# Sharing the casts of v between two engines, one bank pair for batch 1's kv, and another order of stores and loads in SyncE's queue

## The chip, the cores and the metric

The kernel runs on one core of one Trainium2 chip. A core has five engines that run side by side, each through its own list of instructions in order: TensorE (PE in the profile; its weight loads are PEld), VectorE (DVE), ScalarE (ACT), GpSimd (POOL) and SyncE (SP), which issues most of the DMAs. They wait for each other by semaphores. The metric is the device time of one execution in microseconds (us), and the number quoted is the median of several executions.

## What is computed

The program is a linear attention followed by a two-layer network over every token. There are 8 batches of 8 heads, 576 tokens and a head width of 64; the model width is 512 and the hidden width 2048. Cut to what matters, the reference is:

```python
def phi(x): return np.where(x > 0, x, np.exp(x) - 1.0) + 1.0
q_p, k_p = phi(q), phi(k)
kv  = np.einsum('bhsd,bhse->bhde', k_p, v)      # one 64x64 matrix a head
z   = np.sum(k_p, axis=2)
num = np.einsum('bhsd,bhde->bhse', q_p, kv)
den = np.einsum('bhsd,bhd->bhs', q_p, z)[..., None] + 1e-06
x   = (num / den)                                # tokens x 512
h   = x @ w_in                                   # 512 -> 2048
g   = 0.5*h*(1 + tanh(sqrt(2/pi)*(h + 0.044715*h**3)))
out = g @ w_out                                  # 2048 -> 512
```

All inputs and the output are float32 in memory. The kernel computes its matrix products in bf16 and sums them in float32.

## The kernel before

**Tiling.** Of every batch the first 512 tokens form one group; the last 64 tokens of all 8 batches together form a ninth group. `iteration(j)` does the network for group j: 16 steps "h" (one 128-wide block of the hidden width each, four matmuls of 128x512, L385, and a gelu on ScalarE, L395) and 16 or more steps "o" (four or two matmuls into one of four token tiles, L726). Each step has a slot number. The attention of later batches is laid between these steps: `at(j, slot, fn)` notes that fn is to be written out after the given slot of iteration j, and `run` calls it there. So the order of the instructions on every engine is the order in which the Python code writes them; nothing reorders them later.

**Attention of one batch.** q and k go through phi: an exp on ScalarE (L219), a `max(x + 1, 1)` on VectorE (L227), and a minimum of the two (L233). v is cast to bf16 (`cast_v_paired`, L238) into a tile `vp` that has a column of ones beside each head's 64 columns, so that the product with k also gives the sum of k. The kv matmuls (`kv_paired`, L249) run over J = 9 pieces of 64 tokens, for four blocks u of two heads each. Their results stand in PSUM and are copied out into `kvbd`, a block-diagonal bf16 tile (`kv_evac`, L261). Then for each of four chunks of 128 tokens, q (transposed) is multiplied by kvbd (`nab`, L265, tile `n_ps`), VectorE divides (L282, L283), and the result x is transposed into `xt`, the operand of the h steps.

**PSUM.** It has two pools here: `bank` hands out one of six single banks, and `pair_of_banks` the one pair of two neighbouring banks, which is one tile. The pair is used by `nab` for n_ps, and by some batches for kv. Whoever takes it next has to wait until the tile before has been read.

**The start.** `first_batch` prepares batch 0 with nothing beside it but a few matmuls that keep TensorE going (`keep_warm`). v's four blocks come in two halves, `halves[0]` and `halves[1]`; both are cast by VectorE. Kv of the first half goes to two single banks, kv of the second half to the pair, from which VectorE copies the upper 64 partitions and ScalarE the lower 64.

**Batch 1** is prepared by `plan_second` within iteration 0: the transposes of q at slot 23 with two copies by ScalarE (L536), the cast of v by VectorE followed by a cast of a piece of w_out (L145), kv at slot 27 in two single banks, one copied out by VectorE, the other by ScalarE, and n from slot 29 on.

**Loads and stores.** Loads go through SyncE's queue, in the order written. The staging tiles of q, k, v and of the two weight matrices share one pool of seven buffers. Ahead of everything stand the loads for batches 0 to 3 and the weights; later batches' loads are written out by `at`. Transposes by DMA (of q, and of x from batch 2 on) go through the same queue. Stores of the output tiles `o_sb` are issued by ScalarE (L715); the two of group 0 wait until slot 2 of iteration 1.

Of the kernel before, what the change touches and what calls it, by code (L numbers as in the profile page):

```python
# [15 lines left out]
def kernel(  # L16
# [16 lines left out]
    nc = tc.nc  # L33

    B, H, S, D = q.shape
    d_model, d_ff = moe_w_in.shape
    P = 128
# [4 lines left out]
    NP = H // 2  # L42
# [66 lines left out]
    def load_all_pairs(name, src, b):  # L109
        ld_tile(name, b)  # L110
        load_pairs(name, src, b)
# [58 lines left out]
    load_w_out(2, slice(2, 4))  # L170
    load_w_out(3, slice(0, 2))
    load_w_out(3, slice(2, 4))
    for b in (2, 3):
        load_q(b)
        load_all_pairs("k", k, b)
        load_all_pairs("v", v, b)

# [54 lines left out]

    def cast_v_paired(b, us, fn):
        fn(  # L238
            out=vp_paired(b)[:, :, us, 0:D].rearrange("p j u d -> p u j d"),
            in_=ld["v", b][:, us].rearrange("p u (j d) -> p u j d", d=D),  # L240
        )

    def kv_paired(b, ii, kv_of):
# [168 lines left out]
    def first_batch():  # L412
        w_ps = bank("w_ps", [P, 512])

        def keep_warm(n):
            for _ in range(n):
                nc.tensor.matmul(w_ps, lhsT=warm[:, 0:P], rhs=warm)  # L417

        qt = pt.tile([P, C, NP, P], BF16, name="qt")
        qs = (slice(0, 4), slice(4, 8))  # L420

        def transpose_q(s, fn):
            t_ps = bank("t_ps", [P, C, 2, P], BF16)
            for i in range(2):
                for c in range(C):
                    h = 4 * s + 2 * i
                    nc.tensor.transpose(
                        t_ps[:, c, i, :], phi["q", 0][:, c, h : h + 2, :], ident
                    )
            fn(out=qt[:, :, 2 * s : 2 * s + 2, :], in_=t_ps)  # L430

        keep_warm(18)
        for s in range(2):
            for n, hs in (("q", qs[s]), ("k", halves[s])):
                exp_of(n, 0, hs)
                linear_of(n, 0, hs)
                least_of(n, 0, hs)
        transpose_q(0, nc.scalar.copy)
        keep_warm(8)
        transpose_q(1, nc.scalar.copy)  # L440
        keep_warm(5)
        for ii in range(2):
            cast_v_paired(0, halves[ii], nc.vector.tensor_copy)
        kv_ps = [bank("kv_ps", [P, E]) for _ in range(2)]
        kv_paired(0, 0, lambda a, ii: kv_ps[a])
        for a, fn in enumerate((nc.vector.tensor_copy, nc.scalar.copy)):
            kv_evac(0, slice(2 * a, 2 * a + 1), kv_ps[a].rearrange("p (i e) -> p i e", i=1), fn)
        keep_warm(1)
        kv_ps = pair_of_banks("kv_ps")
        kv_paired(0, 1, lambda a, ii: kv_ps[:, a, 0:E])  # L450
        kv_evac(0, slice(1, 4, 2), kv_ps[:, :, 0:E], nc.vector.tensor_copy, nc.scalar.copy)
        for fs in (slice(0, 128), slice(128, 256), slice(256, 512)):
            cast_w_in(0, nc.gpsimd.tensor_copy, fs)
        cast_w_in(1, nc.gpsimd.tensor_copy, slice(256, 512))
        for i in range(2, 4):
            cast_w_in(i, nc.gpsimd.tensor_copy)
        for i in range(2):
            cast_w_out(i, nc.gpsimd.tensor_copy)

        xts[0] = pt.tile([P, NP, MAIN], BF16, name="xt")  # L460
        x = {0: x_tile()}

        def t(c, blocks=range(NP)):
            transpose_x(x[c], xt_chunk(0, c), nc.scalar.copy, blocks)

        def h(m, c, blocks=range(KM)):
            h_begin(0, m, slice(P * c, P * (c + 1)), blocks)

        first, second = range(2), range(2, 4)
        nab_half(x[0], qt[:, 0], 0)  # L470
        nab_half(x[0], qt[:, 0], 1)
        x[1] = nab(qt[:, 1], 0)
        t(0, first)
        h_begun[0][0] = bank("h_ps", [P, MAIN])
        nc.tensor.matmul(h_begun[0][0], lhsT=warm[:, 0:P], rhs=warm, skip_group_check=True)
        t(0, second)
        for m in range(2):
            h(m, 0, first)
        x[2] = nab_in_banks(qt[:, 2], 0)
        h(0, 0, second)  # L480
        t(1)
        h(1, 0, second)
        x[3] = nab(qt[:, 3], 0)
        cast_w_in(1, nc.vector.tensor_copy, slice(0, 256))
        h(2, 0)
        h(3, 0)
        t(2)
        for m in range(3):
            h(m, 1)
        t(3)  # L490
        gelu_table()
        h(3, 1)
        for c in (2, 3):
            for m in range(4):
                h(m, c)
# [16 lines left out]
    def plan_second():  # L512
        b = 1
        x = {}

        def maps():
            for n in "qk":
                exp_of(n, b)
            cast_w_out(2, nc.scalar.copy, slice(0, 2))
            for n in "qk":  # L520
                linear_of(n, b)
            for n in "qk":
                least_of(n, b)

        def transpose_q():
            qts[b] = pt.tile([P, C, NP, P], BF16, name="qt")
            for s in range(2):
                t_ps = bank("t_ps", [P, 2, NP, P], BF16)
                for c in range(2):
                    for i in range(NP):  # L530
                        nc.tensor.transpose(  # L531
                            t_ps[:, c, i, :],
                            phi["q", b][:, 2 * s + c, 2 * i : 2 * i + 2, :],
                            ident,
                        )
                nc.scalar.copy(qts[b][:, 2 * s : 2 * s + 2], t_ps)  # L536

        def casts():
            cast_v_paired(b, slice(0, NP), nc.vector.tensor_copy)
            cast_w_out(2, nc.vector.tensor_copy, slice(2, 4))  # L540

        def kv():
            kv_ps = [bank("kv_ps", [P, 2, E]) for _ in range(2)]
            for ii in range(2):
                kv_paired(b, ii, lambda a, ii: kv_ps[a][:, ii, :])
            for a, fn in enumerate((nc.vector.tensor_copy, nc.scalar.copy)):
                kv_evac(b, slice(2 * a, 2 * a + 2), kv_ps[a], fn)

        def last_w_out():
            for m, fn in enumerate((nc.gpsimd.tensor_copy, nc.scalar.copy) * 2):  # L550
                cast_w_out(3, fn, slice(m, m + 1))
            gelu_table()

        def n(c):
            x[c] = (nab_in_banks if c == 1 else nab)(qts[b][:, c], b)

        def t(c):
            if c == 0:
                xts[b] = pt.tile([P, NP, MAIN], BF16, name="xt")
            transpose_x(x[c], xt_chunk(b, c), nc.scalar.copy)  # L560

        at(0, 15, maps)
        at(0, 23, transpose_q)
        at(0, 23, casts)
        at(0, 27, kv)
        at(0, 27, last_w_out)
        at(0, 29, n, 0)
        at(0, 29, n, 1)
        at(0, 32, n, 2)
        at(0, 32, t, 0)  # L570
        at(0, 33, t, 1)
        at(0, 33, n, 3)
        at(0, 34, t, 2)
        at(0, 34.5, t, 3)
        at(0, 35, h_begin, b, 0, slice(0, 3 * P))
        at(0, 35, h_begin, b, 0, slice(3 * P, MAIN))
# [4 lines left out]
    def plan_third():  # L581
        def n(c):
            transposed_x(2, c, nab(qts[2][:, c], 2))

        for i, name in enumerate("qk"):
            at(1, 2 + i, linear_of, name, 2)
            at(1, 7, exp_of, name, 2)
        at(1, 4, cast_v, 2)
        at(1, 7, gelu_table)
        at(1, 9, least_q, 2)  # L590
        at(1, 10, load_all_pairs, "k", k, 4)
        at(1, 11, least_of, "k", 2)
        at(1, 16, kv_in_pair, 2)
        for c in range(C):
            at(1, 18 + 2 * c, n, c)
# [15 lines left out]
    def plan_prepare(j):  # L611

        b = j + 2
        has_k = b + 1 < B
        at(j, 10 if j == 2 else 4, cast_v, b)
        if has_k:
            at(j, 14 if j == 2 else 12, linear_of, "k", b + 1)
        at(j, 13, linear_of, "q", b)
        at(j, 15, exp_of, "q", b)
        at(j, 20, least_q, b)  # L620
        if has_k:
            at(j, 15, exp_of, "k", b + 1)
            at(j, 22, least_of, "k", b + 1)
# [74 lines left out]
    def finish(j, t, o_ps):  # L698
# [12 lines left out]
        if t % 2 == 1:  # L711
            ov = out[j * S : j * S + MAIN, :].rearrange("(p c) f -> p c f", c=C)[:, t - 1 : t + 1]

            def store():
                nc.scalar.dma_start(out=ov, in_=o_sb)  # L715

            if j == 0:
                at(1, 2, store)
            else:
                store()  # L720

    def o_mm(o_ps, g, t, ms, fs=slice(0, d_model), half=None):
        for m in ms:
# [59 lines left out]
        plan_rest(m)  # L783
    for b in range(3, B + 1):
        plan_attention(b)
    at(1, 26, load_all_pairs, "v", v, 4)
    at(1, 26, load_q, 4)
    for b in range(5, B):
        at(b - 3, 1, load_all_pairs, "k", k, b)
# [40 lines left out]
```

## Time and profile before

| what | value |
|---|---|
| device time, median of 4 runs | 283.76 us (283.67 to 284.01) |
| the profiled execution's own time | 283.77 us |
| its span, first to last instruction | 282.0 us |
| TensorE busy | 273.7 us |
| ScalarE busy | 164.4 us |
| VectorE busy | 102.7 us |
| GpSimd busy | 15.0 us |
| moved by DMA | 53.81 MB, 191 GB/s on average |

The profile is one execution on the chip. Times within it count from its first instruction. In a line of the timeline the first number is the start, the second the duration, then come engine, line of the kernel, operation, output<-input, shapes, how many, and in brackets the idle time of the engine just before and what ended it. In a line of waits the numbers are the total in us, how often, and the longest. The chain that ended last is followed back from the last instruction through whatever released each step. Records of a few matmuls are missing, so a count of 3 can stand for 4.

### The profile page before, as it was taken

The page shows a single profiled execution, that of the slowest core. Times are in us where ns is not written, and L with a number is a line of the kernel's source. Part 1 is how long each engine was busy: PE and PEld are TensorE (multiplying, and loading weights), DVE is VectorE, ACT ScalarE, POOL GpSimd, SP SyncE. Part 2 cuts the span into 40 slices and gives each one's busy share as a digit, 9 for nine tenths or more (in the row PEclk, how much of TensorE's full clock was granted, in tenths as well). Part 3 has the DMA queues.
Part 4 walks back from the last instruction along what each step waited for, and adds up shares of the span by engine and source line. Part 5 has one row for each costly group of instructions (what it writes and reads, how often), then busy time and mean ns, then how long its engine had stood idle before and what let it go on. Part 6 is the DMA issues. An engine that isn't in the chain of part 4 may idle for free.

```text
span 282.0 us, 5115 instructions
## 1 busy us (share of the span) xinstructions
PE 273.7 (97%) x2151; PEld 135.1 (48%) x2181; DVE 102.7 (36%) x177; ACT 164.4 (58%) x224; POOL 15.0 (5%) x21
## 2 busy tenths in 40 slices
PE   8899999999999999999999999999999999999995
PEld 3584455445444544454445444544444444444444
DVE  3850286434955750356034640350124001400001
ACT  4778878785987915692569346833682364026400
POOL 3148200000000000000000000000000000000000
PEclk9999999999999999999999999999999999999999
DMA  7999999977999767916794540056305300430022
GB/s 246 401 406 397 411 402 403 404 253 219 188 358 294 269 170 208 379 28 167 193 390 106 152 131 2 2 151 172 88 2 149 112 2 0 118 108 0 0 77 74
DMA packets 59590, 53.81 MB, mean 191 GB/s; under 512 B 35760, under 2 KB 45360, under 8 KB 59568
## 3 DMA queue, kind: packets, MB, share of 16 engines
q1 hardware_dynamic: 56784, 44.58, 50.8%
q10 hardware_dynamic: 2784, 8.91, 8.8%
q8 instruction: 17, 0.28, 0.4%
q14 instruction: 5, 0.04, 0.0%
HBM read 36.70 MB, written 9.44 MB: 164 GB/s over the span
## 4 chain that ended last, share of the span: by engine, by line
PE 93%; DMA 3%; issue 1%; SPq 1%; DVE 1%; ACT 0%
PE h_ps L385 44%; PE o_ps L726 44%; DMA v_x<-in_v_dram 3%; PE n_ps L323 1%; PE n_ps L249 1%; PE kv_ps L249 1%; PE n_ps L265 1%; PE t_ps L378 1%; SPq L95 1%; SPq L100 0%; PE t_ps L531 0%; DVE vp L238 0%; DVE x L368 0%; DVE kvbd L261 0%; DVE o_sb L687 0%
## 5 line engine op out<-in xcount | busy, mean ns | idle before, releaser
L726 PE MATMUL o_ps<-w_out_sb,g 128*128 128x512 bf16 (+2 forms) x588 | 126.0, 367 | 1.6 <-issue 0.9
L385 PE MATMUL h_ps<-xt,w_in_sb 128*128 128x512 bf16 (+1 forms) x556 | 113.2, 359 | 0.5 <-issue 0.2
L395 ACT ACTIVATE g<-h_ps 128x512 bf16<-128x512 f32 x144 | 84.6, 599 | 36.3 <-PE h_ps L385 34.9
L385 PEld LDWEIGHTS <-w_in_sb 128*128 128x128 bf16 x628 | 58.5, 98 | 64.6
L726 PEld LDWEIGHTS <-g 128*128 128x128 bf16 x608 | 57.4, 98 | 63.4
L687 ACT COPY o_sb<-o_ps 128x512 f32<-128x512 f32 (+1 forms) x19 | 10.8, 576 | 65.4 <-PE o_ps L726 52.3
L687 DVE COPY o_sb<-o_ps 128x512 f32<-128x512 f32 (+1 forms) x19 | 12.2, 646 | 50.3 <-PE o_ps L726 45.5
L282 DVE RECIPROCAL r<-n_ps 128x6 f32<-128x6 f32 (+2 forms) x43 | 8.2, 192 | 60.9 <-PE n_ps L323 55.4
L227 DVE TENSOR_SCALAR k_p<-k_x 128x2304 bf16<-128x2304 f32 (+1 forms) x9 | 11.0, 1222 | 24.5 <-DMA k_x<-in_k_dram 24.5
L283 DVE TENSOR_TENSOR xs<-n_ps,r 128x384 bf16<-128x384 f32 (+1 forms) x30 | 17.5, 584 | 1.0
L219 ACT ACTIVATE k_e<-k_x 128x2304 bf16<-128x2304 f32 (+1 forms) x9 | 17.1, 1903 | 0.9 <-DMA k_x<-in_k_dram 0.9
L219 ACT ACTIVATE q_e<-q_x 128x2048 bf16<-128x2048 f32 (+1 forms) x9 | 15.5, 1720 | 3.0 <-DMA q_x<-in_q_dram 2.9
L227 DVE TENSOR_SCALAR q_p<-q_x 128x2048 bf16<-128x2048 f32 (+1 forms) x9 | 9.9, 1103 | 13.2 <-DMA q_x<-in_q_dram 13.2
L385 PE MATMUL h_ps<-xt_rest,w_in_sb 128*128 128x512 bf16 x63 | 13.9, 379 | 0.1
L233 DVE TENSOR_TENSOR q_p<-q_p,q_e 128x2048 bf16<-128x2048 bf16 (+1 forms) x9 | 9.9, 1102 | 6.9 <-ACT q_e L219 6.8
L408 ACT ACT_TABLE_LOAD x9 | 11.5, 1283 | 0.2
L233 DVE TENSOR_TENSOR k_p<-k_p,k_e 128x2304 bf16<-128x2304 bf16 (+1 forms) x9 | 11.0, 1221 | 1.2 <-ACT k_e L219 1.0
L238 DVE CAST vp<-v_x 128x2304 bf16<-128x2304 f32 (+1 forms) x9 | 11.0, 1224 | 0.5 <-DMA v_x<-in_v_dram 0.3
L417 PE MATMUL w_ps<-warm 128*128 128x512 bf16 x31 | 9.7, 477 | 1.2 <-DVE warm L181 1.2
L219 ACT ACT_TABLE_LOAD x8 | 10.3, 1283 | 0.1
L139 POOL CAST w_in_sb<-w_st 128x512 bf16<-128x512 f32 (+2 forms) x6 | 7.6, 1271 | 15.0 <-DMA w_st<-in_moe_w_in_dram 15.0
L283 DVE TENSOR_TENSOR x<-n_ps,r 128x512 bf16<-128x512 f32 (+1 forms) x13 | 7.9, 609 | 0.4
(50 smaller groups left out, 76.1 us busy)
## 6 DMA issues: line engine op xcount, KB each, us to landing
out_dram<-o_sb ACTq DMA_DIRECT2D x16, 512.0 KB, 3.6
k_x<-in_k_dram SPq DMA_DIRECT2D x7, 1152.0 KB, 7.0
v_x<-in_v_dram SPq DMA_DIRECT2D x7, 1152.0 KB, 11.9
q_x<-in_q_dram SPq DMA_DIRECT2D x6, 1024.0 KB, 11.9
w_st<-in_moe_w_in_dram SPq DMA_DIRECT2D x3, 1024.0 KB, 13.6
q_x<-in_q_dram SPq DMA_DIRECT2D x4, 512.0 KB, 8.6
w_st<-in_moe_w_out_dram SPq DMA_DIRECT2D x2, 1024.0 KB, 12.5
w_st<-in_moe_w_out_dram SPq DMA_DIRECT2D x4, 512.0 KB, 11.2
```

What stands on the lines that cost most here:

```text
L219: nc.scalar.activation(o, i, AF.Exp)
L227: nc.vector.tensor_scalar(o, i, 1.0, 1.0, op0=ALU.add, op1=ALU.max)
L233: nc.vector.tensor_tensor(p, p, e, op=ALU.min)
L238: fn(out=vp_paired(b)[:, :, us, 0:D].rearrange("p j u d -> p u j d"), in_=ld["v", b][:, us].rearrange("p u (j d) -> p u j d", d=D),)
L282: nc.vector.reciprocal(r, n_v[heads + (D,)])
L283: nc.vector.tensor_tensor(x_v, n_v[heads + (slice(0, D),)], r[heads + (None,)].to_broadcast(shape + [D]), op=ALU.mult,)
L385: nc.tensor.matmul(h_ps[:, ts], lhsT=w_in_sb[:, c, P * m : P * (m + 1)], rhs=xt[:, c, ts], start=(c == 0), stop=(c == KM - 1), skip_group_ ...
L395: nc.scalar.activation(g[:, m, :], h_ps, AF.Gelu_apprx_tanh)
L408: nc.scalar.preload_act_table_set("gelu_apprx_tanh_and_others")
L417: nc.tensor.matmul(w_ps, lhsT=warm[:, 0:P], rhs=warm)
L687: (nc.scalar.copy if on_scalar else nc.vector.tensor_copy)(dst, src)
L726: nc.tensor.matmul(o_ps, lhsT=g[:, m, P * t : P * (t + 1)], rhs=w_out_sb[:, m, fs], start=(m == 0), stop=(m == MM - 1),)
```

## The change

Five things are altered. The cast of the second half of v of batch 0, and the cast of v of batch 1, are cut by token pieces: VectorE does pieces 0 to 5 and ScalarE pieces 6 to 8; for batch 1 ScalarE's part stands between its two copies of q. ScalarE alone copies out both parts of kv of batch 0's second half. Batch 1's kv takes the bank pair in place of two single banks. The two stores of group 0 are issued by SyncE, behind the load of q of batch 3, and k of batch 3 is loaded behind them. v of batch 3 is loaded in iteration 1 at slot 26, just ahead of v of batch 4; and VectorE's first step on k of batch 5 moves from slot 14 to slot 18 of iteration 2.

```diff
@@ loads ahead of everything
-    for b in (2, 3):
-        load_q(b)
-        load_all_pairs("k", k, b)
-        load_all_pairs("v", v, b)
+    load_q(2)
+    load_all_pairs("k", k, 2)
+    load_all_pairs("v", v, 2)
+    load_q(3)
@@ the cast
-    def cast_v_paired(b, us, fn):
+    def cast_v_paired(b, us, fn, js=slice(0, J)):
         fn(
-            out=vp_paired(b)[:, :, us, 0:D].rearrange("p j u d -> p u j d"),
-            in_=ld["v", b][:, us].rearrange("p u (j d) -> p u j d", d=D),
+            out=vp_paired(b)[:, js, us, 0:D].rearrange("p j u d -> p u j d"),
+            in_=ld["v", b][:, us].rearrange("p u (j d) -> p u j d", d=D)[:, :, js],
         )
@@ first_batch
-        for ii in range(2):
-            cast_v_paired(0, halves[ii], nc.vector.tensor_copy)
+        cast_v_paired(0, halves[0], nc.vector.tensor_copy)
+        cast_v_paired(0, halves[1], nc.vector.tensor_copy, slice(0, 6))
+        cast_v_paired(0, halves[1], nc.scalar.copy, slice(6, J))
...
-        kv_evac(0, slice(1, 4, 2), kv_ps[:, :, 0:E], nc.vector.tensor_copy, nc.scalar.copy)
+        kv_evac(0, slice(1, 4, 2), kv_ps[:, :, 0:E], nc.scalar.copy)
@@ plan_second, transpose_q, casts and kv
                 nc.scalar.copy(qts[b][:, 2 * s : 2 * s + 2], t_ps)
+                if s == 0:
+                    cast_v_paired(b, slice(0, NP), nc.scalar.copy, slice(6, J))
...
-            cast_v_paired(b, slice(0, NP), nc.vector.tensor_copy)
+            cast_v_paired(b, slice(0, NP), nc.vector.tensor_copy, slice(0, 6))
...
-            kv_ps = [bank("kv_ps", [P, 2, E]) for _ in range(2)]
+            kv_ps = pair_of_banks("kv_ps")
             for ii in range(2):
-                kv_paired(b, ii, lambda a, ii: kv_ps[a][:, ii, :])
+                kv_paired(b, ii, lambda a, ii: kv_ps[:, a, E * ii : E * (ii + 1)])
             for a, fn in enumerate((nc.vector.tensor_copy, nc.scalar.copy)):
-                kv_evac(b, slice(2 * a, 2 * a + 2), kv_ps[a], fn)
+                src = kv_ps[:, a, 0 : 2 * E].rearrange("p (i e) -> p i e", e=E)
+                kv_evac(b, slice(2 * a, 2 * a + 2), src, fn)
@@ plan_third, plan_prepare
+        at(1, 3, load_all_pairs, "k", k, 3)
...
-            at(j, 14 if j == 2 else 12, linear_of, "k", b + 1)
+            at(j, 18 if j == 2 else 12, linear_of, "k", b + 1)
@@ finish
-            def store():
+            if j == 0:
+                at(1, 2, nc.sync.dma_start, ov, o_sb)
+            else:
                 nc.scalar.dma_start(out=ov, in_=o_sb)
-
-            if j == 0:
-                at(1, 2, store)
-            else:
-                store()
@@ the later loads
-    at(1, 26, load_all_pairs, "v", v, 4)
+    for b in (3, 4):
+        at(1, 26, load_all_pairs, "v", v, b)
     at(1, 26, load_q, 4)
```

## The prediction

> **What bounds the kernel now.** I read the page's busy shares first, then the chain that ended last, then TensorE's waits, and last the timeline at the two places where batches 0 and 1 are prepared.
>
> ```profile
> span 282.0 us, 5115 instructions
> PE 273.7 (97%) x2151; PEld 135.1 (48%) x2181; DVE 102.7 (36%) x177; ACT 164.4 (58%) x224; POOL 15.0 (5%) x21
> PE 93%; DMA 3%; issue 1%; SPq 1%; DVE 1%; ACT 0%
> ...
> PE kv_ps L249 <- DVE vp L238: 0.7, 2, 0.4
> PE n_ps L359 <- ACT kvbd L261: 0.4, 1, 0.4
> PE t_ps L378 <- DVE x L368: 0.2, 1, 0.2
> ```
>
> TensorE is busy in 97% of the span and is 93% of the chain; the granted clock is 1.0 throughout. Apart from the wait for its first operand's memset, its only waits for another engine (the last three lines) are in the start-up, before 15 us. After that it never stands still, so a microsecond that it gains or loses anywhere passes to the end unchanged. VectorE, ScalarE, GpSimd and the DMAs count only where they make TensorE wait. The start-up, in order of time (start, duration, engine, line):
>
> ```profile
> 3.39 8.39 DMA v_x<-in_v_dram
> ...
> 11.80 0.76 DVE L238 CAST vp<-v_x 128x1152 bf16<-128x1152 f32 x1
> 12.62 0.48 PE L249 MATMUL kv_ps<-vp,k_p 64*64 64x65 bf16 x36 [0.39 <-DVE vp L238]
> 13.16 0.29 DVE L261 CAST kvbd<-kv_ps 64x130 bf16<-64x130 f32 x1 [0.22 <-PE kv_ps L249]
> 13.48 0.26 ACT L261 CAST kvbd<-kv_ps 64x130 bf16<-64x130 f32 x1 [0.67 <-DVE kvbd L261]
> 13.79 0.27 PE L359 MATMUL n_ps<-kvbd,qt 128*128 128x130 bf16 x2 [0.43 <-ACT kvbd L261]
> ```
>
> v's second half lands at 11.78; VectorE casts it; TensorE's kv matmuls wait; then the two copies out of kv's bank pair run one behind the other, ScalarE 0.03 us after VectorE has ended. Batch 1, which has two separate banks today:
>
> ```profile
> 38.47 1.37 DVE L238 CAST vp<-v_x 128x2304 bf16<-128x2304 f32 x1 [0.34 <-DMA v_x<-in_v_dram]
> 39.81 0.69 DVE L145 CAST w_out_sb<-w_st 128x1024 bf16<-128x1024 f32 x1
> 39.89 0.78 PE L249 MATMUL kv_ps<-vp,k_p 64*64 64x65 bf16 x72
> 40.60 1.04 PE L726 MATMUL o_ps<-w_out_sb,g 128*128 128x512 bf16 x3
> 40.79 0.60 DVE L261 CAST kvbd<-kv_ps 64x130 bf16<-64x130 f32 x2 [0.29 <-PE kv_ps L249]
> 40.81 0.54 ACT L261 CAST kvbd<-kv_ps 64x130 bf16<-64x130 f32 x2 [1.09 <-PE kv_ps L249]
> 41.47 0.63 PE L265 MATMUL n_ps<-kvbd,qt 128*128 128x130 bf16 x8
> ```
>
> Here the two engines copy at the same time, end at 41.39 and 41.35, and n of chunk 0 starts at 41.47, where TensorE arrives anyway. Nothing waits, but every step is in time by less than 0.1 us.
>
> **What the Trainium skill says.** "PSUM — Partial Sum Buffer", section "PSUM bank collisions raise a hardware error": two engines may not touch one bank and quadrant of partitions at once, while different banks run clean; the software has to keep them apart. Here the program keeps them apart by whole tile: the trace has the pair's two copies in sequence (13.45, then 13.48), and the copies of two tiles together (40.79 and 40.81). "DMA: Bandwidth & Descriptors", section "Queues, rings and completion order": SP and ACT each own one row of rings on the same 16 DMA engines; each ring is drained in its order, and rows take turns. The trace agrees: the two stores that ScalarE issues at 50.48 and 51.30 land only 6.7 and 7.9 us later, in a stretch where the DMAs move 388 to 428 GB/s for SyncE's loads.
>
> **The change, part by part.** *v of batch 0.* VectorE's f32 casts take 0.761 us for 1152 elements and 1.357 for 2304, so 0.165 + 0.000517 each; ScalarE's (L145) take 0.618 for 512 and 1.029 for 1024, so 0.207 + 0.00080 each. VectorE's six ninths (768) take 0.56: 11.80 to 12.36. ScalarE's 384 take 0.51 behind its qt copy (10.92 + 1.02 = 11.94), so at most to 12.46; the matmuls that read them are the last third. TensorE can start at 12.41; the keep-warm matmul before it (about 0.21, after the first half ends at 12.23) allows 12.44. That is 0.18 earlier than 12.62. The kv copies follow 0.54 after the start: 12.98. Both are ScalarE's now, 2 x 0.264, to 13.51; n at 13.56 instead of 13.79. From there the chain to the transposes (VectorE's r and x) is what it was, and VectorE has 0.29 less to do. So TensorE gains 0.23 us here. W_in is no obstacle (its first casts end 0.6 us before their matmuls).
>
> *v of batch 1.* TensorE then comes to kv at about 39.66. VectorE's 1536 elements take 0.96: 38.47 to 39.43. ScalarE's 768 take 0.82 behind its first qt copy (about 37.6 to 38.5): ready by 39.4 for the last third. So kv starts on arrival. Its second qt copy slips to about 40.3 and is not read until chunk 2, past 43.6. But the next o matmuls need w_out, whose cast starts with its landing, not with VectorE's being free: it stays at 39.81 + 0.69 = 40.50, matmul at 40.55. Of the 0.23 gained only 0.05 is left there, and TensorE reaches n at 41.42.
>
> *Batch 1's kv in the bank pair.* kv ends 0.23 earlier, so VectorE's two copies run 40.56 to 41.16. In the order of the changed program ScalarE's first copy waits for VectorE's last, and n of chunk 0, whose tile is the same bank pair, waits for ScalarE's last copy before its first matmul. ScalarE: 41.16 + 0.03 + 0.54 = 41.73; n at 41.78. Before: 41.47. This new wait is 0.36 us of standing TensorE. Behind it on ScalarE stand two w_out casts, which end about 0.4 later and have 0.3 to 0.5 of room, plus TensorE's own delay. From here on everything follows TensorE, so **the net is 41.78 - 41.47 = +0.31 us**. Bounds: with no start-up gain at all the serial copies give +0.53; with the copies side by side after all, -0.05.
>
> *Stores on SyncE's queue.* Two issues of 0.39 and 0.34 leave ScalarE (50.48 to 51.64), where they lay under TensorE's h work (ScalarE waits 0.68 for TensorE right after): worth nothing, and at most these 0.73 us if ScalarE set the pace there. SyncE now stands from 42.3 until o_sb is filled at 48.4 to 49.0, with k of batch 3 and batch 2's transposes behind. The ring still holds work until about 53.5 then (q issued at 40.43 lands 13.0 later), so the DMAs don't run dry; k of batch 3 lands near 59 as today (42.40 + 16.5), for a cast at 72.01. The transposes wait for VectorE until 59.87 anyway. Cost nothing.
>
> *v of batch 3 later.* It is issued where batch 4's v stood, 73.36 + 0.31 = 73.67, and the two loads behind it (v, q of batch 4) move back by one load, 2.9 us (1.18 MB at some 400 GB/s). The v issued at that place today lands in 5.9 us:
>
> ```profile
> v_x<-in_v_dram SPq DMA_DIRECT2D x1, 1152.0 KB, 5.9
> ...
> 78.08 1.36 DVE L238 CAST vp<-v_x 128x2304 bf16<-128x2304 f32 x1
> 81.41 0.78 PE L249 MATMUL kv_ps<-vp,k_p 64*64 64x65 bf16 x72
> ```
>
> So it lands at 79.57, the cast runs to 80.95, and TensorE needs it at 81.72: 0.7 us of room where there were 2.0. Next in line: batch 4's v near 82.5 for a cast at 85.46, its q near 85 for VectorE at 86.73; batch 3's transposes near 91 (88.1 today) for TensorE at 93.45; k of batch 5 near 94, which is why its VectorE step stands at slot 18 now, behind the attention; ScalarE's exp of it starts at 95.55. The x transposes of 95.39 to 101.3 are wanted at 107.0 and may end a microsecond or two later. The DMA share falls to 0.2 to 0.6 from 96 to 101, where the backlog is worked off. All hidden; cost nothing, and what it costs when the cover is gone is the first rival.
>
> **Sum.** Profiled execution: span 282.0, own time 283.77, so 1.77 around it, which no edit touches. 282.0 + 0.31 = 282.3, own time 284.08; it lies 0.01 above the median 283.76. I predict **284.1 us**. A measurement of this kernel can tell 0.2% (0.57 us) from no change, so this counts as the same.
>
> **Rivals.** *Slower: v of batch 3 late.* If its load shares the engines with the v queued behind it, instead of going first, both land after 5.9 + 2.9 us, near 82.5; cast to 83.8; TensorE stands about 2.2 us at kv, and the time is 286.3. It decides from a landing later than 80.3. For it: only 0.7 us of room, and four transposes just ahead in the queue. Against it: at the start loads issued together land one after another, and the same place gives 5.9 today with a q queued behind.
>
> *The start-up gain is kept.* If the pair's copies do not hold TensorE, the w_out cast still does: -0.05, 283.7. Against it: the 0.67 that ScalarE waits for VectorE in batch 0's pair.
>
> *No gain at the start.* If ScalarE's cast, or its two copies, take what VectorE saved, the whole +0.53 of the serial copies is left: 284.3.
>
> *Faster by over 0.57 us* has no mechanism that I can see: the three waits shown above add up to 1.3 us, and the landing of v at 11.78 fixes most of them.
>
> **Numbers.** The forecast (+0.2 to +0.5) 0.60, no start-up gain 0.12, gain kept 0.10, v late or another transfer late (each microsecond past its room is one of TensorE) 0.16, something faster 0.02. The range from 283.6 to 285.0 leaves out the late v and the faster end; the likeliest case alone is 283.9 to 284.3. Slower by over 0.2%: the 0.16 of late transfers and a tail of the no-gain case, 0.20; faster 0.04; same 0.76.
>
> **What would show it.** Right: kv of batch 0's second half starts near 12.44 and n at 13.56; in batch 1 ScalarE's copies start just after VectorE's end, near 41.2, and a wait of n_ps (L265) for ScalarE's kvbd of 0.3 to 0.5 us appears among TensorE's waits, which has none there now; v of batch 3 lands by 80.3. Wrong: ScalarE's copies beside VectorE's at 40.6; a wait of kv_ps for vp near 81.7; or a wait on transposes at 93 or 107.

## The result, and the profile after

| kernel | median | range | executions |
|---|---|---|---|
| before | 283.78 us | 283.52 to 284.13 | 53 |
| changed | 284.22 us | 283.96 to 284.52 | 35 |

The ratio is 1.0016, with a 95% interval of 1.0012 to 1.0021: a loss of 0.44 us (0.16%), below the 0.2% at which the prediction draws its line, but clearly not zero. The profiled execution took 284.08 us, against 283.77 for that of before. 284.1 was predicted.

The page of the changed kernel:

```profile
span 282.3 us, 5118 instructions
PE 273.9 (97%) x2151; PEld 135.0 (48%) x2181; DVE 102.0 (36%) x176; ACT 165.7 (59%) x227; POOL 15.0 (5%) x21
PE 88%; DMA 5%; DVE 3%; issue 1%; SPq 1%; ACT 0%; ACTq 0%; DVEq 0%
```

and its waits of TensorE (total in us, times, longest):

```profile
PE n_ps L265 <- ACT kvbd L261: 0.5, 1, 0.5
PE n_ps L359 <- ACT kvbd L261: 0.4, 1, 0.4
PE kv_ps L249 <- DVE vp L238: 0.3, 1, 0.3
```

TensorE's busy time is what it was; its share of the chain fell from 93% to 88%, the rest now running through DMAs and VectorE: between 94 and 106 us the chain passes over VectorE's divisions and a transpose of x by DMA, which lands at 106.03, 0.04 us ahead of TensorE's next piece. TensorE loses no time there: at 93.74 and at 107.31 it is as far behind the kernel before (93.45 and 107.01) as it already was at batch 1. Among the waits, the one at kv of the start has shrunk from 0.7 in two pieces to 0.3 in one, and n_ps at L265 waits for ScalarE's kvbd, which it didn't before. The timeline of the changed kernel at the start:

```profile
11.69 0.56 DVE L238 CAST vp<-v_x 128x768 bf16<-128x768 f32 x1
11.73 0.53 ACT L238 CAST vp<-v_x 128x384 bf16<-128x384 f32 x1
...
12.36 0.48 PE L249 MATMUL kv_ps<-vp,k_p 64*64 64x65 bf16 x36 [0.25 <-DVE vp L238]
12.90 0.54 ACT L261 CAST kvbd<-kv_ps 64x130 bf16<-64x130 f32 x2 [0.22 <-PE kv_ps L249]
13.49 0.27 PE L359 MATMUL n_ps<-kvbd,qt 128*128 128x130 bf16 x2 [0.43 <-ACT kvbd L261]
```

The two casts run side by side (0.56 and 0.53 us for the 0.76 of one engine), and n follows at 13.49 instead of 13.79. The timeline around batch 1:

```profile
38.19 0.96 DVE L238 CAST vp<-v_x 128x1536 bf16<-128x1536 f32 x1 [0.35 <-DMA v_x<-in_v_dram]
38.40 0.85 ACT L238 CAST vp<-v_x 128x768 bf16<-128x768 f32 x1
...
39.53 0.70 DVE L145 CAST w_out_sb<-w_st 128x1024 bf16<-128x1024 f32 x1 [0.37 <-DMA w_st<-in_moe_w_out_dram]
39.55 0.78 PE L249 MATMUL kv_ps<-vp,k_p 64*64 64x65 bf16 x72
40.28 1.02 PE L728 MATMUL o_ps<-w_out_sb,g 128*128 128x512 bf16 x3
40.47 0.60 DVE L261 CAST kvbd<-kv_ps 64x130 bf16<-64x130 f32 x2 [0.24 <-PE kv_ps L249]
41.17 0.54 ACT L261 CAST kvbd<-kv_ps 64x130 bf16<-64x130 f32 x2 [1.03 <-DVE kvbd L261]
41.77 0.63 PE L265 MATMUL n_ps<-kvbd,qt 128*128 128x130 bf16 x8 [0.47 <-ACT kvbd L261]
```

ScalarE's copies start 0.10 us after VectorE's have ended, and TensorE stands 0.47 us at n. It begins n at 41.77 instead of 41.47 and keeps this distance of 0.30 to the end of the span (282.3 instead of 282.0). Of the later loads, the DMA issues of SyncE between 75 and 80 us (count, size, us from issue to landing):

```profile
v_x<-in_v_dram SPq DMA_DIRECT2D x1, 1152.0 KB, 8.0
q_x<-in_q_dram SPq DMA_DIRECT2D x1, 1024.0 KB, 15.2
```

and VectorE's timeline:

```profile
79.89 1.36 DVE L238 CAST vp<-v_x 128x2304 bf16<-128x2304 f32 x1 [1.43 <-DMA v_x<-in_v_dram]
90.54 1.23 DVE L227 TENSOR_SCALAR q_p<-q_x 128x2048 bf16<-128x2048 f32 x1 [3.56 <-DMA q_x<-in_q_dram]
```

Batch 3's v is cast from 79.89 to 81.25, 0.45 us before TensorE's kv at 81.70. Batch 4's v took 8.0 us, its q 15.2; VectorE waits 3.56 us for that q. No wait of TensorE comes of any of it.

### The profile page after: what moved, and what is told of

Read it like the earlier page. It is cut to its first block, busy times and chain, and to the rows that moved or that the text cites. A ratio compares the mean times of both kernels' runs of the same rounds, so it can differ in the third digit from the quotient of the medians.

```text
span 282.3 us, 5118 instructions
## 1 busy us (share of the span) xinstructions
PE 273.9 (97%) x2151; PEld 135.0 (48%) x2181; DVE 102.0 (36%) x176; ACT 165.7 (59%) x227; POOL 15.0 (5%) x21
## 3 DMA queue, kind: packets, MB, share of 16 engines
q1 hardware_dynamic: 57072, 45.62, 53.5%
## 4 chain that ended last, share of the span: by engine, by line
PE 88%; DMA 5%; DVE 3%; issue 1%; SPq 1%; ACT 0%; ACTq 0%; DVEq 0%
PE h_ps L385 44%; PE o_ps L728 40%; DMA v_x<-in_v_dram 3%; DMA xt<-xs 2%; PE n_ps L323 1%; PE kv_ps L249 1%; PE n_ps L265 1%; DVE xs L283 1%; PE n_ps L249 1%; PE t_ps L378 1%; SPq L95 1%; DVE k_p L227 0%; ACT kvbd L261 0%; SPq L100 0%; DVE o_sb L692 0%
## 5 line engine op out<-in xcount | busy, mean ns | idle before, releaser
L238 DVE CAST vp<-v_x 128x2304 bf16<-128x2304 f32 (+3 forms) x9 | 10.4, 1158 | 1.9 <-DMA v_x<-in_v_dram 1.8
```

What stands on the lines that cost most here:

```text
L238: fn(out=vp_paired(b)[:, js, us, 0:D].rearrange("p j u d -> p u j d"), in_=ld["v", b][:, us].rearrange("p u (j d) -> p u j d", d=D)[:, :, js],
```

## The experiments

The first runs set the prediction's account (the two copies in line behind each other cost, the start gives back a part, the order of loads and stores is free) against one in which the reordered loads or stores have a share in the loss. The later ones ask what e2 and e5 had shown.

All ratios are to runs of the kernel before on the same chip (its medians were 283.57, 283.61, 283.58 and 283.57 in the four sessions). In the comparison above it had 283.78, so times of different sessions are not subtracted from each other: where a run is set against the changed kernel, it is by their distances from the kernel before, which is 0.44 us for the changed kernel.

| run | what it is | median | ratio, 95% interval |
|---|---|---|---|
| e1 | changed, pair copied by VectorE alone | 283.65 | 1.0004 (0.9996 to 1.0012) |
| e2 | changed, loads and stores of before | 285.63 | 1.0071 (1.0057 to 1.0085) |
| e3 | before, new loads and stores | 283.61 | 1.0002 (0.9994 to 1.0010) |
| e4 | before, batch 1's kv in the pair | 284.24 | 1.0022 (1.0013 to 1.0031) |
| e5 | before, start's casts and copies | 286.49 | 1.0102 (1.0086 to 1.0117) |
| e6 | changed, q transpose in the pair instead of kv | 283.47 | 0.9995 (0.9987 to 1.0003) |
| e7 | e6, loads and stores of before | 285.16 | 1.0054 (1.0042 to 1.0067) |
| e8 | changed, batch 3's v behind batch 4's | 285.70 | 1.0074 (1.0061 to 1.0088) |
| e9 | before, 2 tiny copies on ScalarE | 289.27 | 1.0201 (1.0186 to 1.0216) |
| e10 | e5, 12 tiny copies on ScalarE | 285.98 | 1.0084 (1.0069 to 1.0099) |
| e11 | e7, 12 tiny copies on ScalarE | 285.97 | 1.0090 (1.0073 to 1.0107) |
| e12 | e11, the tile they write enlarged | 283.55 | 0.9999 (0.9991 to 1.0007) |

### One part at a time

**e1: one engine copies the pair.** `kv_in_pair` is the kernel's function for later batches: the same matmuls into the pair, and one copy out by VectorE.

```diff
         def kv():
-            kv_ps = pair_of_banks("kv_ps")
...
-            for a, fn in enumerate((nc.vector.tensor_copy, nc.scalar.copy)):
-                src = kv_ps[:, a, 0 : 2 * E].rearrange("p (i e) -> p i e", e=E)
-                kv_evac(b, slice(2 * a, 2 * a + 2), src, fn)
+            kv_in_pair(b)
```

> The changed kernel, but VectorE alone copies batch 1's kv out of the bank pair, in two pieces of 64x260 (0.43 us each for batch 2 today). Theory A (the serial copies VectorE, then ScalarE, are what costs): they end at 40.47 + 0.86 = 41.33, n of chunk 0 starts at 41.38 instead of 41.77, and the time falls by 0.39 from the changed kernel's 284.22 to about 283.83, +0.02% against the kernel before. Rival (what costs is sharing the pair with n, or the casts of v, whoever copies): n stays near 41.7 and the time near 284.2.

283.65 us, 0.08 above before, which is within the interval. In its profile n of batch 1 starts at 41.28 and the wait for ScalarE's kvbd is gone:

```profile
40.35 0.87 DVE L658 CAST kvbd<-kv_ps 64x260 bf16<-64x260 f32 x2
```

kv still stands in the pair, so it is not the pair as such that costs, but that two engines empty it one behind the other: their four copies take from 40.47 to 41.71 in the changed kernel, 1.24 us, and VectorE's two larger ones 0.87. This run alone can't tell the second engine from the greater number of copies; e6, further down, has the four copies again.

**e4: the pair alone**, on the kernel before (the diff of batch 1's kv shown with the change, and nothing else).

> The kernel before with only batch 1's kv in the bank pair, copied by VectorE and then ScalarE. Theory A: ScalarE's copies run at 41.42 to 41.96, n of chunk 0 starts at 42.0 instead of 41.47, +0.53 us, about 284.3. Rival: the pair costs nothing by itself and the time stays at 283.8.

284.24 us, 0.67 above before. Its waits of TensorE show the new one in the same place:

```profile
PE n_ps L265 <- ACT kvbd L261: 0.5, 1, 0.5
```

This one edit costs more than the whole change. e1 and e4, with e6, settle where the loss is.

**e3: the new loads and stores alone**, on the kernel before (the diffs of the loads, of `finish` and of the slot 18).

> The kernel before with only the stores and loads in the new order. Theory A: no difference, within 0.1 us of the kernel before. Theory B: +0.14 us. In both, q of batch 4 lands near 90 and v of batch 3 near 79.6, with TensorE's kv of batch 3 not waiting.

283.61 us: nothing can be told from before, so in the kernel before the order of loads and stores is free as far as this can be told (the interval ends at +0.28 us). That leaves room for the 0.14 of theory B; but in e4, which has the old order, the median lies 0.13 above the profiled execution too (284.24 and 284.11), so that distance needs no late transfers.

**e8: batch 3's v behind batch 4's**, on the changed kernel.

```diff
-    for b in (3, 4):
+    for b in (4, 3):
         at(1, 26, load_all_pairs, "v", v, b)
```

> The changed kernel with v of batch 3 one load later still, behind v of batch 4. The rival of the prediction priced: v of batch 3 lands near 82.7 instead of 79.9, VectorE's cast ends near 84.1, TensorE stands at batch 3's kv from 81.7 to 84.1, and the time is 2.4 us above the changed kernel: 286.6. If v's landing were not what kv waits for, 284.2.

285.70 us, 2.09 above before, so about 1.6 above the changed kernel. The waits of TensorE, and VectorE's timeline:

```profile
PE kv_ps L249 <- DVE vp L238: 2.2, 2, 1.7
```

```profile
81.90 1.36 DVE L238 CAST vp<-v_x 128x2304 bf16<-128x2304 f32 x1 [3.62 <-DMA v_x<-in_v_dram]
```

The cast starts 2.0 us later than in the changed kernel (79.89), and TensorE stands 1.7 us in one piece at that kv. So the rival of a late v was a real price, and the room of 0.45 us in the changed kernel is what separates it from that. The expectation was too large because it took the second load's landing from the changed kernel (82.72): here both loads were issued 0.6 us earlier and landed at 78.95 and 81.88, again 2.9 us apart.

**e6: another tile in the pair**, a version meant to keep the gain: batch 1's kv goes back to two single banks, and the second half of its q transposes uses the pair instead, which has one reader.

```diff
-                t_ps = bank("t_ps", [P, 2, NP, P], BF16)
+                if s == 0:
+                    t_ps = bank("t_ps", [P, 2, NP, P], BF16)
+                else:
+                    t_pair = ps_a.tile([P, 2, 1024], BF16, name="t_ps", tag="a")
+                    t_ps = t_pair[:, 0].rearrange("p (c i n) -> p c i n", c=2, i=NP)
...
-            kv_ps = pair_of_banks("kv_ps")
+            kv_ps = [bank("kv_ps", [P, 2, E]) for _ in range(2)]
...
```

> The changed kernel with batch 1's kv in two single banks again, and the second half of its transposed q in the bank pair instead. Theory A: the two engines copy kv at the same time, 40.5 to 41.1, n of chunk 0 starts on TensorE's arrival at 41.15 to 41.2, and the start's gain of 0.3 us reaches the end: about 283.5 to 283.6, below both kernels. Rival (the start's gain is lost elsewhere, at w_out's cast or the late transfers): 283.8.

283.47 us; n at 41.27, no wait for kvbd. The same four copies as in the changed kernel run side by side:

```profile
40.42 0.60 DVE L261 CAST kvbd<-kv_ps 64x130 bf16<-64x130 f32 x2
40.44 0.54 ACT L261 CAST kvbd<-kv_ps 64x130 bf16<-64x130 f32 x2 [0.33 <-PE kv_ps L249]
```

It removes the loss. Against before it is 0.14 lower, and the interval includes 1, so it isn't shown to be faster. Little of the start's gain reaches n of batch 1 here: from the first kv to it are 29.68 us, and 29.70 in e3, whose start is that of before. The prediction's working had that too (w_out's cast starts with its landing): 0.05 of 0.23 was to be left.

### Two surprises with the old order of loads

**e2: the changed kernel with the loads and stores of before** (the reverse of e3's diffs).

> The changed kernel with the stores, the loads of k and v of batch 3 and VectorE's step on k of batch 5 put back as before; start and batch 1 stay changed. Theory A (the order of the transfers is hidden): no difference to the changed kernel, 284.1 to 284.2, n of chunk 0 near 41.8. Theory B (late transfers between 80 and 107 us cost the 0.14 us by which the changed kernel's median lies above its profiled execution): 284.08, and transposes for group 3 land by 105 instead of 106.5.

**e5: the start's edits alone**, on the kernel before.

```diff
...
-        for ii in range(2):
-            cast_v_paired(0, halves[ii], nc.vector.tensor_copy)
+        cast_v_paired(0, halves[0], nc.vector.tensor_copy)
+        cast_v_paired(0, halves[1], nc.vector.tensor_copy, slice(0, 6))
+        cast_v_paired(0, halves[1], nc.scalar.copy, slice(6, J))
...
-        kv_evac(0, slice(1, 4, 2), kv_ps[:, :, 0:E], nc.vector.tensor_copy, nc.scalar.copy)
+        kv_evac(0, slice(1, 4, 2), kv_ps[:, :, 0:E], nc.scalar.copy)
```

> The kernel before with only batch 0's part: v's second half cast by two engines, and both copies of its kv by ScalarE. Theory A: TensorE's transposes of the first x come 0.2 to 0.3 us earlier than 14.80, but batch 1's kv still has to wait for VectorE's cast of v, whose start is set by the landing of v, so that TensorE waits there and nothing is left at the end: within 0.1 us of the kernel before. Rival (a gain at the start passes to the end): -0.25 us, about 283.5.

**e7: e6 with the loads and stores of before.**

> As the run before it, with the stores and loads in the old order too. Theory A (transfers are hidden): the same as that run. Theory B (late transfers cost 0.14): 0.14 us less than that run, about 283.4.

All three were expected to change next to nothing, and came out at 285.63, 286.49 and 285.16: 2.1, 2.9 and 1.6 us above before, the first of them 1.6 above the changed kernel. In each, n of batch 1 starts when it should; the time goes later, between 54 and 65 us. The waits of TensorE in e5:

```profile
PE o_ps L727 <- ACT g L395: 1.4, 1, 1.4
PE kv_ps L249 <- DVE k_p L233: 1.3, 1, 1.3
```

ScalarE's timeline of the kernel before in that stretch (the line's second number is the time of two issues with the gap between them):

```profile
50.48 1.17 ACTq L715 DMA_DIRECT2D out_dram<-o_sb  x2
51.69 1.08 ACT L395 ACTIVATE g<-h_ps 128x512 bf16<-128x512 f32 x2 [0.68 <-PE h_ps L385]
```

and of e5:

```profile
50.52 5.24 ACTq L716 DMA_DIRECT2D out_dram<-o_sb  x2
55.80 2.56 ACT L395 ACTIVATE g<-h_ps 128x512 bf16<-128x512 f32 x5 [5.06 <-issue]
58.37 1.28 ACT L219 ACT_TABLE_LOAD   x1
```

The first of group 0's two stores took 4.75 us to issue, where it takes 0.39 in the kernel before. ScalarE's gelus stand behind it, and the exp of batch 2's k behind them, so first an o matmul waits and then batch 2's kv. In e2 the issue took 3.82 us, in e7 3.93. The semaphores that the store waits for are set by 50.74 in e5's trace, 0.2 us after its start, and SyncE's loads were issued within 0.2 us of where e4 has them, whose store took 0.38. What differs is ScalarE's stream: the three have two more instructions ahead of the store. Another coincidence: in the DMA queues, one 8 KB packet of kind "instruction" passes 1.5 to 1.8 us before the store is through. In e5, from 53.5 to 54.5 us:

```profile
q1 hardware_dynamic: 182, 0.39, 101.4%
q14 instruction: 1, 0.01, 1.9%
```

**e9: two instructions more and nothing else.** On the kernel before:

```diff
     nc.vector.memset(warm, 0.0)
+    spare = const.tile([P, 2], BF16, name="spare")
+    for i in range(2):
+        nc.scalar.copy(spare[:, i : i + 1], warm[:, i : i + 1])
```

> Two runs with the old order of loads and stores and a split cast lost 1.6 to 2.9 us where ScalarE's first store of group 0 took 3.8 to 4.8 us to issue instead of 0.39 us. In each of them the store stood two instructions later in ScalarE's stream than in the kernel before, and an 8 KB packet of the instruction queue (queue 14) landed 1.5 to 1.8 us before the store was through. This run is the kernel before with two one-element copies put first on ScalarE, in its idle time ahead of the first load. Theory F (a store issued at that place of the stream waits for the fetch of further instructions): the store takes some 4 us, the end is 2.3 to 3.0 us later than before, 285.9 to 286.6. Theory G (the split of v and its new release of the staging buffer does it): the store takes 0.39 us and the time is that of before, 283.5 to 283.8.

289.27 us, more than either theory gave. The store's part is there: ScalarE's timeline, and TensorE's:

```profile
52.99 5.73 ACTq L718 DMA_DIRECT2D out_dram<-o_sb  x2
58.77 1.57 ACT L398 ACTIVATE g<-h_ps 128x512 bf16<-128x512 f32 x3 [5.55 <-issue]
```

```profile
59.42 6.43 PE L729 MATMUL o_ps<-w_out_sb,g 128*128 128x512 bf16 x29 [1.88 <-ACT g L398]
68.00 0.78 PE L252 MATMUL kv_ps<-vp,k_p 64*64 64x65 bf16 x72 [1.29 <-DVE k_p L236]
```

The first store took 5.24 us, and the instruction packet passes at 56.48, 1.75 before its end. From n of batch 1 to batch 2's kv the kernel loses 3.4 us (2.2 late at the one, 5.6 at the other). There is no split cast in this kernel, so theory G falls: the split is not needed for the long issue. The other 2.2 us are lost earlier and were not expected.

**e10 and e11: twelve instructions more**, which moves the store away from that place; the same edit with 12 in place of 2, on e5 and on e7.

> The run that had only the start's split cast and ScalarE's copies added to the kernel before (286.5), with twelve one-element copies put first on ScalarE in its idle time. Theory F: the fetch is asked for some 6 us ahead of the store and is over by then; the store takes about 0.4 us, and the time is before less the start's gain of 0.2 to 0.3: 283.2 to 283.5. Theory G: 286.5 as without the copies.

> The run with batch 1's second half of the q transposes in the bank pair and the loads and stores of before (285.16), with twelve one-element copies put first on ScalarE. Theory F: the store takes about 0.4 us and the time is as with the new order of loads, 283.2 to 283.6. Theory G: 285.2 as without the copies.

285.98 and 285.97 us: as totals, theory F missed as well. But the store is free again, as ScalarE's timeline of e10 shows, and neither wait of e5 is left: the kernel loses nothing between n of batch 1 and batch 2's kv (2.0 us late at both).

```profile
52.42 0.60 ACT L398 ACTIVATE g<-h_ps 128x512 bf16<-128x512 f32 x1 [0.27 <-PE h_ps L388]
52.48 0.86 ACTq L719 DMA_DIRECT2D out_dram<-o_sb  x2
```

Its instruction packet passes at 46.81, 5.7 us ahead of the store. The 2 us are lost before 44 us, as in e9 (n of batch 1 starts at 43.47, and at 43.67 there), and with them go slower loads. The stretch from 13 to 40 us in e11 (busy times, clock, DMA share, GB/s):

```profile
13.00:40.00 27.00, 25.47 (x218) 14.36 (x204) 9.54 (x18) 20.16 (x29) 11.34 (x8) 1.00 1.06 381
```

The kernel before has 405 GB/s there, e9 and e10 380 and 381. The granted clock is not the cause: it is 1.00 here and in e10 (0.94 in e9's profile). The small tile `spare` of 4 or 24 bytes sits ahead of the staging buffers in the on-chip memory. The traces hold no addresses; by the compiled programs, as the expectation below has it, the staging buffers begin 32 bytes past a multiple of 64 with this tile and on such a multiple without.

**e12: the tile made 1,024 bytes long**, so that the staging buffers are back on multiples of 64; otherwise e11.

```diff
-    spare = const.tile([P, 12], BF16, name="spare")
+    spare = const.tile([P, 512], BF16, name="spare")
```

> The run with twelve one-element copies on ScalarE, q transposes in the bank pair, and loads and stores of before (285.97), but with the small tile that the copies write made 1,024 bytes long instead of 24. In the three runs with the small tile the loads ran at about 380 GB/s instead of 405 between 13 and 40 us, and the compiled programs put the staging buffers behind that tile at addresses 32 bytes past a multiple of 64; 1,024 bytes put them back on multiples of 64. Theory F with this: loads at 405 GB/s again, the store takes 0.4 us, 8 KB of instructions fetched near 46 us, and the time is 283.1 to 283.5. If the slower loads have another cause that comes with the copies: 285.9 to 286.0. If the store's long issue has another cause than the fetch, so that it comes back once the loads have their pace again: 285.2, as without the copies.

283.55 us. The same stretch, the queues from 44.0 to 44.6 us, and ScalarE's timeline:

```profile
13.00:40.00 27.00, 26.39 (x256) 15.24 (x257) 10.95 (x19) 21.90 (x31) 11.36 (x8) 1.00 1.05 405
```

```profile
q14 instruction: 1, 0.01, 3.2%
```

```profile
50.11 0.87 ACTq L725 DMA_DIRECT2D out_dram<-o_sb  x2
```

The loads have their pace, the packet passes at 44.23, the two stores take 0.87 us in all, and the time is that of before, 1.6 us under e7 (and 0.05 over theory F's range, which counted on a gain from the start). So e7's loss was the store's long issue, undone by moving the store in ScalarE's stream; and the loss of e11 came from where the tiles lie, since the length of `spare` is all that differs. No group of engine instructions differs in its median by more than 0.01 us between the two profiles, so it is the transfers that became slower.

What is shown: two more instructions ahead of the store bring the long issue, with or without the split cast, and twelve take it away. What is not: that the fetch of instructions is what the store waits for. The packet moves with ScalarE's instruction count (52 to 56 us with none or two added, 44 to 47 with twelve), and in all four runs with the long issue the store is through 1.5 to 1.8 us after it; but the kernel before issues its second store as the 64th instruction of ScalarE in its trace, in 0.34 us, and those four have their first store at that same place. The changed kernel's packet passes at 52.63, and the gelus near it wait for TensorE alone, 0.27 us each. Why a first store waits there and these don't stays open.

## Why the prediction was right

*What bounds the kernel.* Right. What TensorE lost at batch 1's n in the changed kernel (0.30 us between the two profiles) was still there at the end of the span.

*Start.* kv of the second half was predicted at 12.44 and came at 12.36, n at 13.56 and came at 13.49. But the comparison with 13.79 flatters the step, for the profiled execution of before had its first kv at 11.75, later than the others with its start-up and the loads at full pace (11.53 in e3, 11.47 in e4). Counted from the first kv to n of the second half, before takes 2.03 or 2.04 us (in its own profile, e3, e4) and the changed start 1.87 (changed kernel) or 1.86 (e1). The gain is 0.17, not 0.23.

*Batch 1's v.* Right: 0.96 on VectorE as predicted, 0.85 on ScalarE for 0.82, and kv on arrival. The step that gives the gain away in part (w_out's cast starts with its landing) is to be seen in the bracket of the line at 39.53, which waits for the DMA.

*The pair.* The wait came, for the reason given, in the order given: 41.77 for a predicted 41.78. Its size alone is better taken from e4 and e3: from the first kv to batch 1's n is 30.32 us in e4 and 29.70 in e3, so the pair costs 0.62 where the working had 0.53 to 0.54. Most of the rest is the hand-over: ScalarE started 0.10 us after VectorE's end (0.11 in e4) and not 0.03. Both terms were a little off, each towards a larger loss: 0.62 - 0.17 = 0.45, which is the measured 0.44. That the two profiled executions are just 0.30 apart, beside the predicted 0.31, is luck: before's happened to start 0.13 late. The skill's page "PSUM — Partial Sum Buffer" was read rightly in the prediction: the two halves of the pair are different banks, which its section on collisions lets two engines use at once. It is the order by whole tiles in this program that makes the wait, and e1 (one engine) and e6 (two tiles) remove the wait.

*Loads and stores.* "All hidden; cost nothing" is right for the sum, and e3 shows it alone, to within its interval. Three of its terms were off. Batch 3's v had 0.45 us of room, not 0.7. Batch 4's q was expected at about 85 and landed at 90.52: the step counted SyncE's loads one behind another and left out ScalarE's two stores of group 1, issued at 80.14 and 81.23. The queues from 83 to 90 us (packets, MB, share of the engines' time):

```profile
q1 hardware_dynamic: 1248, 0.86, 80.0%
q10 hardware_dynamic: 287, 1.05, 38.7%
```

ScalarE's queue (q10) moves 1.05 MB while SyncE's (q1), with the q's last and the transposes, moves 0.86. From 86 to 87 us the trace has 74 packets of 1,024 bytes of this load and 80 of 4,096 bytes of the stores. This fits the turn-taking of the section "Queues, rings and completion order" that the prediction itself had cited, and not applied here: turns of one packet are uneven when the packets are. It accounts for some 3 of the 5.5 us, by which time all but about 15 of the load's 1,024 packets had started; these came mostly 0.2 us apart, beside the transposes, up to 89.71, for a reason that no run shows. Third, batch 5's k lands at 97.23 (predicted 94). The last x transpose behind it lands at 106.47, 1.9 us later than before (104.53), within the "microsecond or two" of the prediction, and 0.7 ahead of TensorE's 107.15. It held by little.

*What the prediction could not say.* It weighed the stores' move by ScalarE's own time ("worth nothing, and at most these 0.73 us"). That holds in a kernel whose store is free. With the start's casts in it, the old order costs 1.6 us (e2 against the changed kernel), so the move protects against a loss that another part of the same change would have brought. The parts don't add up: start +2.9 (e5), pair +0.67 (e4), loads 0.0 (e3), all together +0.44. No rival had this.

## What to carry to other kernels

Where two engines are to empty one tile at the same time, look in the trace at whether their copies overlap: here the program orders by tile, and 0.6 us of a bound TensorE hung on it, while one engine, or two tiles, cost nothing that could be told from noise. Don't take an edit that adds an instruction or a few bytes as neutral: look at the issue time of the DMAs that a compute engine issues among its own work, and at the pace of the loads, before a difference is put down to the idea under test. When a load is moved behind others, count the other queues' packets in the same stretch, not only the own queue's order.

## What was not expected of the hardware

- A store of 512 KB issued by ScalarE took 3.82, 3.93, 4.75 and 5.24 us to issue in four kernels with two more instructions ahead of it, and 0.38 or 0.39 us otherwise (before, e4, e10, e11, e12).
- Tiles that lie 32 bytes further on, so that by the compiled programs the staging buffers begin 32 bytes past a multiple of 64, took the loads from 405 to 381 GB/s, 6% less, and made the kernel 2.4 us slower (e11 against e12). The Trainium skill, "DMA: Bandwidth & Descriptors", section "How a descriptor splits into AXI transactions", has it that a descriptor that doesn't start on a multiple of 256 bytes starts with a transaction from the boundary below, and that the bytes ahead of its start are fetched unused and still cost time. An address 32 past a multiple of 64 is never a multiple of 256, and the loss agrees in its sign. But that section speaks of what is read, and the staging buffers are what the loads write: no run shows that its account holds for them, or which boundary counts.
- Two loads of the same size issued 0.6 us apart landed 2.9 us apart (79.86 and 82.72): they went one after another, as the prediction assumed, while batch 4's q and ScalarE's stores shared the engines (1.05 MB of stores beside 0.86 MB from 83 to 90 us).
